# Decode attention with a gated mixer: PV with V as the moving operand, by hand on TensorE

## The chip, the cores and the metric

The kernel runs on one NeuronCore of a Trainium2 chip. The metric is the device time of one execution in microseconds; the median of several runs counts. The engines are named as in the profile: PE (TensorE, with PEld for its weight loads), DVE (VectorE), ACT (ScalarE), POOL (GpSimd) and SP (SyncE, which here only issues transfers). Sixteen DMA engines move data from the main memory (HBM) into the on-chip memory (SBUF). Matmul results go to PSUM.

## What is computed

One new token of width 512 passes through an attention block (32 heads, a cache of 16,384 keys and values per head, head width 128) and, beside it, through a small gated mixer. A scalar gate mixes the two results.

```python
x = A_x                                             # (1, 1, 512)
g = sigmoid((x * gate_w).sum(-1, keepdims=True))

# attention
q = (x @ wq).reshape(1, 1, 32, 128).transpose(0, 2, 1, 3)
scores = einsum('bhqd,bhkd->bhqk', q, k_cache) * 128 ** -0.5
p = softmax(scores)
o = einsum('bhqk,bhkd->bhqd', p, v_cache)
a = o.transpose(0, 2, 1, 3).reshape(1, 1, 4096) @ wo

# mixer (one token)
z = gelu(einsum('bsd,df->bsf', x, w_in))            # 1792 wide
z1, z2 = z[..., :896], layernorm(z[..., 896:])
b = einsum('bsf,fd->bsd', z1 * (w_sp * z2 + b_sp), w_out)

return g * a + (1 - g) * b                          # (1, 1, 512)
```

All inputs are bf16. K and V of one head have 4 MB (4,194,304 bytes) each, so the caches are 64 such loads; wq and wo are another 4 MB each, w_in and w_out 1.8 and 0.9 MB.

## The kernel before

A K or V tile has 128 partitions. Partition p holds the keys p*128 to p*128+127, each with 128 elements, so that every partition reads one run of 32 KB. The whole program is unrolled: no loop is left on the chip.

*Start.* wq is loaded into a buffer of the v tag (L69), then K of heads 0 to 2, V of head 0 and the mixer's weights (L97 to L106). The query is computed with x spread over all columns of the stationary operand, so that every partition has the whole q (`qb`, L116 to L126).

*Scores of head h (`scores`, L210 to L226).* K is done in two halves of 64 keys per partition. VectorE multiplies a half by q in place (L216). PE adds the products up over groups of 8 elements: 16 matmuls with the identity as stationary operand and 512 columns add slices of the product into one PSUM bank (L219). VectorE reduces the remaining 8 (L221). ACT takes the exponent of both halves at once and the row sums with it (L224). The softmax is taken without a maximum; the sums are divided out at the end.

*PV of head h (`attend`, L228 to L232).* 128 matmuls: each loads a block of V (128 keys x 128 elements) as stationary operand and sends one column of p through it. They add up in column h of `o_ps`, which is o in columns.

*Order.* The loop at L237 runs over the heads, two heads ahead with the scores: it loads K of h+2, computes the scores of h+2, loads V of h, and does PV of h. The framework puts each engine's instructions into an order by priority, which follows the program, and by what it takes to be ready; it adds the semaphores itself. K has three buffers and V two (wq and wo take part: wq in a v buffer, wo in a k buffer). All large loads go through SP's queue in one order: V of h waits until PV of h-2 has freed its buffer, and K of h+3 is queued behind V of h+1. The gate (L141) and the mixer (L159) are called after head 1.

*End.* V of head 31 is loaded in three pieces (64, 32 and 32 blocks), wo in three (16, 12 and 4 slices of 512 columns, L253). The sum of all exponents comes from a matmul with ones (L258), o is normalised (L265) and turned from columns into the order in which wo's rows lie on the partitions: a PE transpose (L267), a copy (L269) and four matmuls with a selection matrix (L272). Then 128 matmuls with wo as stationary operand (L278) add to `a_ps`, in which the mixer's part already stands (L204). In each the stationary operand takes every fourth column of wo (`"p (k m c) -> p k m c"`, L255), so that element 4m+c of the output lies in partition m, column c. The result (128 x 4) is cast (L281) and written with 128 runs of 8 bytes (L282).

Of the kernel before, what the change touches and what calls it, by code (L numbers as in the profile page):

```python
# [8 lines left out]
ACT = mybir.ActivationFunctionType  # L9
ALU = mybir.AluOpType  # L10
AX = mybir.AxisListType

FP32 = mybir.dt.float32
BF16 = mybir.dt.bfloat16
# [3 lines left out]
def kernel(  # L18
# [57 lines left out]
    def load_k(h):  # L76
        t = kv.tile([P, NJ * Dh], BF16, name="k_t", tag="k", bufs=3)
        nc.sync.dma_start(out=t[:], in_=k_src[h])  # L78
        ktile[h] = t

    def load_v(h, cuts=()):
        t = kv.tile([P, NJ * Dh], BF16, name="v_t", tag="v")
        edges = [0, *cuts, NJ]
        for a, b in zip(edges[:-1], edges[1:]):
            nc.sync.dma_start(out=t[:, a * Dh:b * Dh], in_=v_src[h][:, a * Dh:b * Dh])  # L85
        vtile[h] = t
# [43 lines left out]
    for i in range(4):  # L130
        nc.vector.tensor_copy(out=sel[:, i, :].rearrange("h (m i) -> h m i", i=4)[:, :, i],
                              in_=ident[0:H, 0:H])

    a_ps = ps_1.tile([P, 512], FP32, name="a_ps")
    o_ps = ps_1.tile([P, H], FP32, name="o_ps")
    g_sb = const.tile([P, 1], FP32, name="g_sb")
# [4 lines left out]
    def gate():  # L141
        gw_ps = ps_m.tile([P, DC + 2], FP32, name="gw_ps", tag="mm")
        for c in range(DC):
            nc.tensor.matmul(gw_ps[:, c:c + 1], lhsT=gw_row[0:1, c::DC], rhs=ones_row[0:1, 0:1],
                             start=True, stop=True)
        nc.tensor.matmul(gw_ps[:, DC:DC + 2], lhsT=ones_row[0:1, :], rhs=wb_row[0:1, :],  # L146
                         start=True, stop=True)
        gw_col = const.tile([P, DC], BF16, name="gw_col")
        nc.vector.tensor_copy(out=gw_col[:], in_=gw_ps[:, 0:DC])  # L149
        nc.vector.tensor_copy(out=wbf[:], in_=gw_ps[:, DC:DC + 2])  # L150
        g_ps = ps_m.tile([P, 1], FP32, name="g_ps", tag="mm")
        for c in range(DC):
            nc.tensor.matmul(g_ps[:, :], lhsT=xb[:, c, :], rhs=gw_col[:, c:c + 1],
                             start=(c == 0), stop=(c == DC - 1))
        nc.scalar.activation(out=g_sb[:], in_=g_ps[:, :], func=ACT.Sigmoid)
        nc.scalar.activation(out=gm_sb[:], in_=g_ps[:, :], func=ACT.Sigmoid, scale=-1.0)


    def mixer():  # L159
        z_ps = ps_m.tile([P, FC], FP32, name="z_ps", tag="mm")  # L160
        w_in5 = w_in[:].rearrange("p c (e m k) -> p c e m k", e=2, k=FhC)
        for fc in range(FC):
            for c in range(DC):
                nc.tensor.matmul(z_ps[:, fc:fc + 1], lhsT=w_in5[:, c, fc // FhC, :, fc % FhC],  # L164
                                 rhs=xb[:, c, 0:1], start=(c == 0), stop=(c == DC - 1))
        z = const.tile([P, FC], FP32, name="z")
        nc.vector.tensor_copy(out=z[:], in_=z_ps[:])  # L167
        t = const.tile([P, FC], FP32, name="t")
        nc.vector.tensor_mul(out=t[:], in0=z[:], in1=z[:])
        nc.vector.tensor_scalar(out=t[:], in0=t[:], scalar1=0.044715, scalar2=1.0,  # L170
                                op0=ALU.mult, op1=ALU.add)
        nc.vector.tensor_mul(out=t[:], in0=t[:], in1=z[:])
        nc.scalar.activation(out=t[:], in_=t[:], func=ACT.Sigmoid, scale=1.5957691216057308)
        nc.vector.tensor_mul(out=z[:], in0=z[:], in1=t[:])
        stats = const.tile([P, 2], FP32, name="stats")
        nc.vector.reduce_sum(out=stats[:, 0:1], in_=z[:, FhC:FC], axis=AX.X)
        sq = const.tile([P, FhC], FP32, name="sq")
        nc.vector.tensor_mul(out=sq[:], in0=z[:, FhC:FC], in1=z[:, FhC:FC])
        nc.vector.reduce_sum(out=stats[:, 1:2], in_=sq[:], axis=AX.X)
        tot_ps = ps_m.tile([P, 2], FP32, name="tot_ps", tag="mm")  # L180
        nc.tensor.matmul(tot_ps[:, :], lhsT=ones_f[:, :], rhs=stats[:, :], start=True, stop=True)
        mv = const.tile([P, 2], FP32, name="mv")
        nc.vector.tensor_scalar(out=mv[:], in0=tot_ps[:, :], scalar1=1.0 / Fh, scalar2=0.0,
                                op0=ALU.mult, op1=ALU.add)
        var = const.tile([P, 1], FP32, name="var")
        nc.vector.tensor_mul(out=var[:], in0=mv[:, 0:1], in1=mv[:, 0:1])
        nc.vector.tensor_sub(out=var[:], in0=mv[:, 1:2], in1=var[:])
        rstd = const.tile([P, 1], FP32, name="rstd")
        nc.scalar.activation(out=rstd[:], in_=var[:], func=ACT.Sqrt, bias=eps_t[:, 0:1], scale=1.0)
        nc.vector.reciprocal(out=rstd[:], in_=rstd[:])  # L190
        z2n = const.tile([P, FhC], FP32, name="z2n")
        nc.vector.tensor_scalar(out=z2n[:], in0=z[:, FhC:FC], scalar1=mv[:, 0:1],
                                scalar2=rstd[:, 0:1], op0=ALU.subtract, op1=ALU.mult)
        nc.vector.tensor_scalar(out=z2n[:], in0=z2n[:], scalar1=wbf[:, 0:1],
                                scalar2=wbf[:, 1:2], op0=ALU.mult, op1=ALU.add)
        uf = const.tile([P, FhC], FP32, name="uf")
        nc.vector.tensor_mul(out=uf[:], in0=z[:, 0:FhC], in1=z2n[:])
        u = const.tile([P, FhC], BF16, name="u")
        nc.vector.tensor_scalar(out=u[:], in0=uf[:], scalar1=gm_sb[:, 0:1], scalar2=0.0,  # L199
                                op0=ALU.mult, op1=ALU.add)  # L200
        w_out4 = w_out[:].rearrange("p k (m c) -> p k m c", c=DC)
        for k in range(FhC):
            for c in range(DC):
                nc.tensor.matmul(a_ps[:, c:c + 1], lhsT=w_out4[:, k, :, c], rhs=u[:, k:k + 1],  # L204
                                 start=(k == 0 and c == 0), stop=False, skip_group_check=True)

    L_sb = const.tile([P, H], FP32, name="L_sb")
    p_sb = {}

    def scores(h):  # L210
        k3 = ktile[h][:].rearrange("p (j d) -> p j d", d=Dh)
        qh = qb[:, h * Dh:(h + 1) * Dh].unsqueeze(1).broadcast_to([P, NH, Dh])
        s_sb = sp.tile([P, NJ], FP32, name="s_sb")
        for s in range(2):
            ks = k3[:, s * NH:(s + 1) * NH, :]
            nc.vector.tensor_tensor(out=ks, in0=ks, in1=qh, op=ALU.mult)  # L216
            s_ps = ps_s.tile([P, NH, W], FP32, name="s_ps")
            for i in range(NS):
                nc.tensor.matmul(s_ps[:, :, :], lhsT=ident[:, :], rhs=ks[:, :, i * W:(i + 1) * W],  # L219
                                 start=(i == 0), stop=(i == NS - 1))  # L220
            nc.vector.tensor_reduce(out=s_sb[:, s * NH:(s + 1) * NH], in_=s_ps[:, :, :],  # L221
                                    axis=AX.X, op=ALU.add)
        p_t = sp.tile([P, NJ], BF16, name="p_t", bufs=4)
        nc.scalar.activation(out=p_t[:], in_=s_sb[:], func=ACT.Exp, scale=inv_sqrt_dh,  # L224
                             accum_out=L_sb[:, h:h + 1])
        p_sb[h] = p_t  # L226

    def attend(h):  # L228
        v3 = vtile[h][:].rearrange("p (j d) -> p j d", d=Dh)
        for j in range(NJ):  # L230
            nc.tensor.matmul(o_ps[:, h:h + 1], lhsT=v3[:, j, :], rhs=p_sb[h][:, j:j + 1],  # L231
                             start=(j == 0), stop=(j == NJ - 1))  # L232

    AHEAD = 2
    scores(0)
    scores(1)
    for h in range(H):  # L237
        if h + AHEAD < H:
            if h > 0:
                load_k(h + AHEAD)  # L240
            scores(h + AHEAD)
        if h > 0:
            load_v(h, cuts=(64, 96) if h == H - 1 else ())
        if h < H - 1:
            attend(h)
        if h == 1:
            gate()
            mixer()


    wo_t = kv.tile([P, H * D], BF16, name="wo_t", tag="k", bufs=3)
    wo_src = A_wo.rearrange("(p k) n -> p (k n)", k=H)
    for a, b in ((0, 16), (16, 28), (28, 32)):  # L253
        nc.sync.dma_start(out=wo_t[:, a * D:b * D], in_=wo_src[:, a * D:b * D])  # L254
    wo4 = wo_t[:].rearrange("p (k m c) -> p k m c", k=H, c=DC)  # L255

    ltot_ps = ps_m.tile([P, H], FP32, name="ltot_ps", tag="mm")
    nc.tensor.matmul(ltot_ps[:, :], lhsT=ones_f[:, :], rhs=L_sb[:, :], start=True, stop=True)  # L258
# [16 lines left out]
    nc.vector.tensor_copy(out=o2[:], in_=o2_ps[:, :])  # L275
    for k in range(H):
        for c in range(DC):
            nc.tensor.matmul(a_ps[:, c:c + 1], lhsT=wo4[:, k, :, c], rhs=o2[:, k:k + 1],  # L278
                             start=False, stop=(k == H - 1), skip_group_check=True)
    res = const.tile([P, DC], BF16, name="res")  # L280
    nc.vector.tensor_copy(out=res[:], in_=a_ps[:, 0:DC])  # L281
    nc.sync.dma_start(out=out.rearrange("a b (p c) -> (a b p) c", c=DC), in_=res[:])  # L282


# [28 lines left out]
```

## Time and profile before

| quantity | us |
|---|---|
| median of 8 runs | 667.06 (666.7 to 667.64) |
| the profiled execution | 667.01 |
| its span, first to last instruction | 665.1 |
| PE busy on scores (L219), all heads | 289.5 |
| PE busy on PV (L231), all heads | 108.4 |
| VectorE busy on products (L216), all heads | 280.5 |
| one half of a product (L216) | 4.42 |
| reducing one half (L221) | 0.69 |
| PV of one head, matmuls (L231) | 3.35 |
| a V load, from issue to landing (median) | 32.3 |
| a K load, from issue to landing (median) | 41.7 |

The span is what the profiler sees between the first and the last instruction. Busy times of different engines overlap and don't add up to the span. Where the profile says "clock 0.50", PE's clock was granted at half its full rate in that stretch. "x16" is the number of instructions merged into a row. In the profile's rows, an arrow with a name at the end tells what ended the wait before it.

In the steady part a head looks like this on the engines (head 29 of 0 to 31, in us from the span's start): K has landed by 580.65, VectorE multiplies until 589.41, PE does the scores from 585.13 to 594.54, PV of head 27 follows from 594.38, and SP issues V of head 29 at 597.82.

### The profile page before, as it was taken

The numbers are of one execution on the slowest core, as the hardware profiler recorded it, in microseconds if no ns is written. First come the engines' busy times: TensorE is split into PE (matmuls) and PEld (weight loads), VectorE is DVE, ScalarE is ACT, GpSimd is POOL, SyncE is SP. The second block draws the span as 40 slices with busy tenths as digits, with TensorE's granted clock in tenths as the row PEclk, the third lists the DMA queues.
The fourth block names the chain that finished last, engine by engine and source line by source line (L and its number), as shares of the span: only waits on it lengthen the run. The fifth ranks groups of instructions, "written<-read, shape, count | busy, mean of one in ns | idle before, by whom it ended". The sixth has DMA issues, their size and how long they took to land.

```text
span 665.1 us, 11264 instructions
## 1 busy us (share of the span) xinstructions
PE 412.9 (62%) x5386; PEld 237.4 (36%) x5386; DVE 330.9 (50%) x162; ACT 25.5 (4%) x81; POOL 0.7 (0%) x6
## 2 busy tenths in 40 slices
PE   2767656567756567664557765557775654776663
PEld 1325333334323334422334432334442333442363
DVE  1593655444655444565544465544455653456500
ACT  0402000000000000000000000000000000000000
POOL 0000000000000000000000000000000000000000
PEclk9898666787656787866787876677876668876665
DMA  9999999999999999999999999999999999999985
GB/s 378 441 429 429 431 429 431 433 426 430 435 427 433 424 435 433 427 431 435 425 431 436 423 429 438 429 427 432 431 428 436 425 430 431 431 432 434 399 353 229
DMA packets 10566, 280.31 MB, mean 421 GB/s; under 512 B 1302, under 2 KB 1304, under 8 KB 1560
## 3 DMA queue, kind: packets, MB, share of 16 engines
q1 hardware_dynamic: 10512, 279.58, 98.0%
q8 instruction: 42, 0.69, 0.4%
q14 instruction: 4, 0.03, 0.0%
q10 hardware_dynamic: 8, 0.00, 0.0%
HBM read 279.58 MB, written 0.00 MB: 420 GB/s over the span
## 4 chain that ended last, share of the span: by engine, by line
DMA 69%; PE 20%; DVE 9%; SPq 1%; issue 0%; DVEq 0%
DMA k_t<-in_A_k_cache_dram 66%; PE s_ps L219 15%; DVE k_t L216 9%; PE o_ps L231 5%; DMA wo_t<-in_A_wo_dram 3%; SPq L85 1%; PE a_ps L278 0%; DVE s_sb L221 0%; SPq L254 0%; SPq L69 0%; PE ltot_ps L258 0%; DVE res L281 0%; SPq L78 0%; DVEq L216 0%
## 5 line engine op out<-in xcount | busy, mean ns | idle before, releaser
L219 PE MATMUL s_ps<-k_t,ident 128*128 128x512 bf16 x1024 | 289.5, 452 | 219.1 <-DVE k_t L216 219.1
L216 DVE TENSOR_TENSOR k_t<-k_t,qb 128x8192 bf16<-128x8192 bf16 x64 | 280.5, 4421 | 149.7 <-DMA k_t<-in_A_k_cache_dram 149.7
L219 PEld LDWEIGHTS <-ident 128*128 128x128 bf16 x1024 | 115.3, 113 | 381.1 <-issue 222.7
L231 PEld LDWEIGHTS <-v_t 128*128 128x128 bf16 x4096 | 108.3, 97 | 14.2 <-DMA v_t<-in_A_v_cache_dram 7.1
L231 PE MATMUL o_ps<-p_t,v_t 128*128 128x1 bf16 x4096 | 108.4, 163 | 6.7 <-DMA v_t<-in_A_v_cache_dram 6.7
L221 DVE TENSOR_REDUCE s_sb<-s_ps 128x64 f32<-128x512 f32 x64 | 44.2, 691 | 127.3 <-PE s_ps L219 127.3
L224 ACT ACTIVATE p_t<-s_sb 128x128 bf16<-128x128 f32 x32 | 9.9, 310 | 586.1 <-DVE s_sb L221 586.1
L121 PE MATMUL q_ps<-wq_t,xb 128*128 128x512 bf16 x32 | 8.8, 443 | 10.3 <-DMA wq_t<-in_A_wq_dram 10.3
L121 PEld LDWEIGHTS <-xb 128*128 128x128 bf16 x32 | 3.5, 110 | 15.4 <-issue 11.7
L278 PE MATMUL a_ps<-o,wo_t 128*128 128x1 bf16 x128 | 4.6, 172 | 4.9 <-DMA wo_t<-in_A_wo_dram 4.9
L265 DVE TENSOR_TENSOR o_sb<-o_ps,rl 128x32 bf16<-128x32 f32 x1 | 0.2, 190 | 13.6 <-PE o_ps L231 13.6
L278 PEld LDWEIGHTS <-wo_t 128*128 128x128 bf16 x128 | 4.4, 118 | 5.1 <-DMA wo_t<-in_A_wo_dram 5.1
L124 DVE CAST qb<-q_ps 128x512 bf16<-128x512 f32 x1 | 0.7, 691 | 11.1 <-PE q_ps L121 11.1
L224 ACT ACTIVATION_READ_ACCUMULATOR p_t<-s_sb 128x1 f32 x32 | 6.0, 187 | 0.0
L281 DVE CAST res<-a_ps 128x4 bf16<-128x4 f32 x1 | 0.2, 163 | 9.3 <-PE a_ps L278 9.3
L126 ACT CAST qb<-q_ps 128x512 bf16<-128x512 f32 x7 | 4.1, 585 | 14.9 <-PE q_ps L121 14.9
L149 DVE CAST gw_col<-gw_ps 128x4 bf16<-128x4 f32 x1 | 0.2, 163 | 6.5 <-PE gw_ps L146 6.5
L164 PE MATMUL z_ps<-xb,w_in 128*128 128x1 bf16 x56 | 3.1, 192 | 0.0
L164 PEld LDWEIGHTS <-w_in 128*128 128x128 bf16 x56 | 3.1, 154 | 0.0
L167 DVE COPY z<-z_ps 128x14 f32<-128x14 f32 x1 | 0.2, 172 | 5.5 <-PE z_ps L164 5.5
L224 ACT ACT_TABLE_LOAD x2 | 2.6, 1283 | 0.0
L204 PE MATMUL a_ps<-u,w_out 128*128 128x1 bf16 x28 | 1.1, 172 | 2.3 <-DVE u L199 2.3
(57 smaller groups left out, 18.7 us busy)
## 6 DMA issues: line engine op xcount, KB each, us to landing
k_t<-in_A_k_cache_dram SPq DMA_DIRECT2D x32, 4096.0 KB, 41.7
v_t<-in_A_v_cache_dram SPq DMA_DIRECT2D x31, 4096.0 KB, 32.8
wq_t<-in_A_wq_dram SPq DMA_DIRECT2D x1, 4096.0 KB, 12.2
v_t<-in_A_v_cache_dram SPq DMA_DIRECT2D x1, 2048.0 KB, 7.8
v_t<-in_A_v_cache_dram SPq DMA_DIRECT2D x2, 1024.0 KB, 10.5
wo_t<-in_A_wo_dram SPq DMA_DIRECT2D x1, 2048.0 KB, 16.7
w_in<-in_B_w_in_dram SPq DMA_DIRECT2D x1, 1792.0 KB, 44.4
wo_t<-in_A_wo_dram SPq DMA_DIRECT2D x1, 1536.0 KB
```

The lines of the kernel that those rows point to most:

```text
L85: nc.sync.dma_start(out=t[:, a * Dh:b * Dh], in_=v_src[h][:, a * Dh:b * Dh])
L121: nc.tensor.matmul(q_ps[:, :], lhsT=xb[:, c, :], rhs=wq[:, c, nb * QB:(nb + 1) * QB], start=(c == 0), stop=(c == DC - 1))
L124: nc.vector.tensor_copy(out=qb[:, 0:QB], in_=q_ps[:, :])
L126: nc.scalar.copy(out=qb[:, nb * QB:(nb + 1) * QB], in_=q_ps[:, :])
L164: nc.tensor.matmul(z_ps[:, fc:fc + 1], lhsT=w_in5[:, c, fc // FhC, :, fc % FhC], rhs=xb[:, c, 0:1], start=(c == 0), stop=(c == DC - 1))
L204: nc.tensor.matmul(a_ps[:, c:c + 1], lhsT=w_out4[:, k, :, c], rhs=u[:, k:k + 1], start=(k == 0 and c == 0), stop=False, skip_group_check=True)
L216: nc.vector.tensor_tensor(out=ks, in0=ks, in1=qh, op=ALU.mult)
L219: nc.tensor.matmul(s_ps[:, :, :], lhsT=ident[:, :], rhs=ks[:, :, i * W:(i + 1) * W], start=(i == 0), stop=(i == NS - 1))
L221: nc.vector.tensor_reduce(out=s_sb[:, s * NH:(s + 1) * NH], in_=s_ps[:, :, :], axis=AX.X, op=ALU.add)
L224: nc.scalar.activation(out=p_t[:], in_=s_sb[:], func=ACT.Exp, scale=inv_sqrt_dh, accum_out=L_sb[:, h:h + 1])
L231: nc.tensor.matmul(o_ps[:, h:h + 1], lhsT=v3[:, j, :], rhs=p_sb[h][:, j:j + 1], start=(j == 0), stop=(j == NJ - 1))
L278: nc.tensor.matmul(a_ps[:, c:c + 1], lhsT=wo4[:, k, :, c], rhs=o2[:, k:k + 1], start=False, stop=(k == H - 1), skip_group_check=True)
```

## The change

- `attend` stays for heads 29 to 31. For heads 0 to 28 it is replaced by `attend_wide` and `collect`. `attend_wide` takes four columns of p as stationary operand (128 x 4) and four blocks of V as moving operand (128 x 512); 32 such matmuls add up in a PSUM tile `d_ps` of 4 x 512. Row r of the tile holds the sum of p's columns 4g+r with all four blocks; only the diagonal blocks (row r, columns r*128 to r*128+127) belong together. ACT copies the tile to SBUF. `collect`, one head later, adds the four diagonal blocks into column h of `o_ps` with four fp32 matmuls against a 4 x 4 identity (`ident_f`, a new tile copied at the start).
- The scores are cut into halves (`scores_half`), with the same instructions.
- PE's instructions in the loop keep the order in which the program states them: first half of the scores of h+2, `collect` of h-1, second half, `attend_wide` of h. For head 29, `attend` stands between the two halves of head 31's scores. Gate and mixer follow `attend_wide` of head 1.
- V of h is now requested before the scores of h+2 in the program. V of head 31 is requested after the loop.
- wo is loaded in four pieces, of 16, 8, 6 and 2 slices. The stationary operands from w_out and wo are blocks of 128 adjacent columns, so that element 128c+m of the output lies in partition m, column c. A PE transpose turns the result into 4 rows of 128, a VectorE copy moves it to SBUF, and the output is written with 4 runs of 256 bytes.

```diff
+    ident_f = const.tile([4, 4], FP32, name="ident_f")
+    nc.vector.tensor_copy(out=ident_f[:], in_=ident[0:4, 0:4])
...
-        w_out4 = w_out[:].rearrange("p k (m c) -> p k m c", c=DC)
+        w_out4 = w_out[:].rearrange("p k (c m) -> p k c m", c=DC)
...
-                nc.tensor.matmul(a_ps[:, c:c + 1], lhsT=w_out4[:, k, :, c], rhs=u[:, k:k + 1],
+                nc.tensor.matmul(a_ps[:, c:c + 1], lhsT=w_out4[:, k, c, :], rhs=u[:, k:k + 1],
...
+    R = 512 // Dh
+    diag = {}
+
+    def attend_wide(h):
+        d_ps = ps_s.tile([R, R * Dh], FP32, name="d_ps")
+        NG = NJ // R
+        for g in range(NG):
+            nc.tensor.matmul(d_ps[:, :], lhsT=p_sb[h][:, g * R:(g + 1) * R],
+                             rhs=vtile[h][:, g * R * Dh:(g + 1) * R * Dh],
+                             start=(g == 0), stop=(g == NG - 1))
+        d_sb = sp.tile([R, R * Dh], FP32, name="d_sb")
+        nc.scalar.copy(out=d_sb[:], in_=d_ps[:, :])
+        diag[h] = d_sb
+
+    def collect(h):
+        for r in range(R):
+            nc.tensor.matmul(o_ps[:, h:h + 1], lhsT=diag[h][:, r * Dh:(r + 1) * Dh],
+                             rhs=ident_f[:, r:r + 1], start=(r == 0), stop=(r == R - 1))
+
     AHEAD = 2
-    scores(0)
-    scores(1)
-    for h in range(H):
-        if h + AHEAD < H:
+    WIDE = H - 3
+    with tc.manual_schedule(engines={mybir.EngineType.PE}):
+        for h in range(AHEAD):
+            scores_half(h, 0)
+            scores_half(h, 1)
+        for h in range(H - 1):
             if h > 0:
-                load_k(h + AHEAD)
-            scores(h + AHEAD)
-        if h > 0:
-            load_v(h, cuts=(64, 96) if h == H - 1 else ())
-        if h < H - 1:
-            attend(h)
-        if h == 1:
-            gate()
-            mixer()
+                if h + AHEAD < H:
+                    load_k(h + AHEAD)
+                load_v(h)
+            if h + AHEAD < H:
+                scores_half(h + AHEAD, 0)
+            if 0 < h <= WIDE:
+                collect(h - 1)
+            if h < WIDE:
+                scores_half(h + AHEAD, 1)
+                attend_wide(h)
+            else:
+                attend(h)
+                if h + AHEAD < H:
+                    scores_half(h + AHEAD, 1)
+            if h == 1:
+                gate()
+                mixer()
+        load_v(H - 1, cuts=(64, 96))
...
-    for a, b in ((0, 16), (16, 28), (28, 32)):
+    for a, b in ((0, 16), (16, 24), (24, 30), (30, 32)):
...
-            nc.tensor.matmul(a_ps[:, c:c + 1], lhsT=wo4[:, k, :, c], rhs=o2[:, k:k + 1],
+            nc.tensor.matmul(a_ps[:, c:c + 1], lhsT=wo4[:, k, c, :], rhs=o2[:, k:k + 1],
...
-    nc.sync.dma_start(out=out.rearrange("a b (p c) -> (a b p) c", c=DC), in_=res[:])
+    rT_ps = ps_m.tile([DC, P], BF16, name="rT_ps", tag="mm")
+    nc.tensor.transpose(rT_ps[:, :], res[:], ident[:])
+    resT = const.tile([DC, P], BF16, name="resT")
+    nc.vector.tensor_copy(out=resT[:], in_=rT_ps[:, :])
+    nc.sync.dma_start(out=out.rearrange("a b (c m) -> (a b c) m", c=DC), in_=resT[:])
```

More of the change, by code (lines that the diff above doesn't have):

```diff
@@ L208, with scores_half @@
     p_sb = {}
-    def scores(h):
+    s_tile = {}
+    def scores_half(h, s):
         k3 = ktile[h][:].rearrange("p (j d) -> p j d", d=Dh)
         qh = qb[:, h * Dh:(h + 1) * Dh].unsqueeze(1).broadcast_to([P, NH, Dh])
[L213 to L226, printed above, removed]
+        if s == 0:
+            s_tile[h] = sp.tile([P, NJ], FP32, name="s_sb")
+        s_sb = s_tile[h]
+        ks = k3[:, s * NH:(s + 1) * NH, :]
+        nc.vector.tensor_tensor(out=ks, in0=ks, in1=qh, op=ALU.mult)
+        s_ps = ps_s.tile([P, NH, W], FP32, name="s_ps")
+        for i in range(NS):
+            nc.tensor.matmul(s_ps[:, :, :], lhsT=ident[:, :], rhs=ks[:, :, i * W:(i + 1) * W],
+                             start=(i == 0), stop=(i == NS - 1))
+        nc.vector.tensor_reduce(out=s_sb[:, s * NH:(s + 1) * NH], in_=s_ps[:, :, :],
+                                axis=AX.X, op=ALU.add)
+        if s == 1:
+            p_t = sp.tile([P, NJ], BF16, name="p_t", bufs=4)
+            nc.scalar.activation(out=p_t[:], in_=s_sb[:], func=ACT.Exp, scale=inv_sqrt_dh,
+                                 accum_out=L_sb[:, h:h + 1])
+            p_sb[h] = p_t
     def attend(h):
@@ L251 @@
     wo_t = kv.tile([P, H * D], BF16, name="wo_t", tag="k", bufs=3)
     wo_src = A_wo.rearrange("(p k) n -> p (k n)", k=H)
-    for a, b in ((0, 16), (16, 28), (28, 32)):
+    for a, b in ((0, 16), (16, 24), (24, 30), (30, 32)):
         nc.sync.dma_start(out=wo_t[:, a * D:b * D], in_=wo_src[:, a * D:b * D])
-    wo4 = wo_t[:].rearrange("p (k m c) -> p k m c", k=H, c=DC)
+    wo4 = wo_t[:].rearrange("p (k c m) -> p k c m", k=H, c=DC)
     ltot_ps = ps_m.tile([P, H], FP32, name="ltot_ps", tag="mm")
```

## The prediction

> **What bounds the kernel now.** I read the busy table first, then the slices, the queue table, the chain of waits, the stages and the order of time at the end.
>
> ```profile
> PE 412.9 (62%) x5386; PEld 237.4 (36%) x5386; DVE 330.9 (50%) x162; ACT 25.5 (4%) x81; POOL 0.7 (0%) x6
> DMA  9999999999999999999999999999999999999985
> GB/s 378 441 429 429 431 429 431 433 426 430 435 427 433 424 435 433 427 431 435 425 431 436 423 429 438 429 427 432 431 428 436 425 430 431 431 432 434 399 353 229
> ...
> q1 hardware_dynamic: 10512, 279.58, 98.0%
> q8 instruction: 42, 0.69, 0.4%
> ...
> DMA 69%; PE 20%; DVE 9%; SPq 1%; issue 0%; DVEq 0%
> ```
>
> No compute engine is full, the 16 DMA engines are in every slice but two, and the chain is 69% transfers. A pair of k and v tiles (8.39 MB) at 431 GB/s takes 19.4 us, the period of a head in the chain (58.2 us per three heads). The chain also shows PE and VectorE 29% of the time, but that is no bound: a v load issued at 557.09 lands a median of 32.3 us later, because two and a bit transfers of 9.7 us are queued ahead of it. About 22 us of queued work therefore covers the path "k lands, product, scores, PV, next v load".
>
> ```profile
> core 0: us, PE busy (x) PEld busy (x) DVE busy (x) ACT busy (x) POOL busy (x), PEclk, DMA share, GB/s
> 622.00:630.00 8.00, 6.03 (x21) 2.40 (x21) 6.85 (x3) 0.00 (x0) 0.00 (x0) 0.66 1.02 438
> 630.00:633.00 3.00, 3.00 (x30) 1.59 (x29) 0.31 (x2) 0.00 (x0) 0.00 (x0) 1.00 0.43 186
> 633.00:636.00 3.00, 3.00 (x119) 3.00 (x116) 0.47 (x1) 0.40 (x2) 0.00 (x0) 1.00 0.61 262
> 636.00:639.00 3.00, 0.27 (x5) 0.16 (x5) 0.60 (x2) 0.00 (x0) 0.00 (x0) 0.78 0.76 279
> 639.00:655.00 16.00, 7.93 (x261) 7.40 (x261) 0.59 (x3) 0.00 (x0) 0.00 (x0) 0.50 1.00 421
> ```
>
> The stage from 630 to 637 is where the loss shows: half of the DMA engines idle. The packet records of the trace say which half. Each load is 128 packets of 32 KB, eight per engine, 1.215 us each. At 630.2 to 631.2 eight engines end v of head 30; the other eight end it at 637.0 to 638.4, some 7 us later, and run on into v of head 31 (issued at 636.3) without a gap. So the late eight are never idle and set the end; an earlier v load alone would only move idle time of the early eight. What makes them late is the other queue: each of the 42 instruction packets (16 KB, about 1.05 us) holds up one engine, and its next data packet takes about 1.7 us instead of 1.215. A fetch costs its engine about 1.05 + 0.5 = 1.55 us. 42 x 1.55 / 8 = 8.1 us, which is the lag. The 42 fetches are TensorE's: 2 x 5386 = 10,772 instructions of 64 bytes are 0.69 MB.
>
> ```profile
> 655.03 2.29 PE L278 MATMUL a_ps<-o,wo_t 128*128 128x1 bf16 x64 [3.51 <-DMA wo_t<-in_A_wo_dram]
> ...
> 658.73 2.29 PE L278 MATMUL a_ps<-o,wo_t 128*128 128x1 bf16 x64 [1.41 <-DMA wo_t<-in_A_wo_dram]
> 661.06 0.16 DVE L281 CAST res<-a_ps 128x4 bf16<-128x4 f32 x1 [9.31 <-PE a_ps L278]
> 661.25 0.35 SPq L282 DMA_DIRECT2D out_dram<-res  x1
> ```
>
> The last data packet ends at 659.49. The second wo piece releases 64 matmuls at 658.73 (the third piece has landed before they are through), and the sum is there at 661.04, 1.55 us after the last packet.
>
> **What the Trainium skill says.** "Runtime: NRT & Kernel Launch", section Instruction fetch mechanics: an engine's instructions are streamed in 16 KiB blocks of 256 by a DMA queue of its sequencer, and the cost is "mostly hidden". The 42 packets of 16 KB agree; hidden it is only from TensorE, for here the DMA engines are the bound. "DMA: Bandwidth & Descriptors", section Queues, rings and completion order: a transfer is split over fixed rings of the 16 engines, and an engine takes turns between rows. That agrees with a lag that never evens out. "TensorE: Matmul & The Clock Gate", Part 1: the clock is half when TensorE has idled for some 3.4 us and full after as long of activity. The trace agrees: 0.50 between heads, 1.00 at the end of the scores; matmuls of 512 columns start 0.426 us apart at first and about 0.216 apart warm (16 in 3.61 us, the last one's latency included).
>
> **The change, part by part.** The profiled execution took 667.01 us for a span of 665.1, so about 1.9 us lie outside; the median of the runs is 667.06, and I carry differences over to it.
>
> *V as moving operand, heads 0 to 28.* Removed: 29 x 128 matmuls with a weight load each. Added: 29 x 32 matmuls of 512 columns, 29 x 4 fp32 ones (two instructions each, as ltot's x2 rows show) and 29 ACT copies (0.58 us by the q copies, on an engine 4% busy: nothing). TensorE's matmuls become 1024 + 928 + 232 + 384 (three narrow heads) + 267 (rest) = 2835, with weight loads 5670 instructions, 22 fetches. 20 fetches fewer x 1.55 / 8 engines = 3.9 us on the late half. Fetches come whole: the latest engine had about 6 of 42 and will have 3 of 22, 4.7 us. I take 4.2; bounds 2.5 (the rest falls unevenly) and 6 (no lag matters).
>
> TensorE pays per head: first half 16 x 0.216 = 3.5 us warm, 6.8 cold; collect 8 small fp32 instructions, 0.6 to 2.4 us by the ltot and tot rows, taken 1; second half 3.5; wide PV 32 x 0.216 = 6.9. That is 14.9 to 18.2 us in a period of 19.4: below the transfers, and shorter idle keeps it warmer. Its cover is narrow, and the rival below prices its loss. VectorE keeps its 2 x 4.42 + 2 x 0.69 = 10.2 us. From k landing to the v buffer coming free: 8.9 us of products, some 5 for the second half behind collect, 6.9 wide = about 20.9, against 16.9 (4.4 + 9.2 + 3.3). The next v and k loads are issued 4 us later, with about 18 us of transfers still queued: hidden. SP's order stays v of h, then k of h+3.
>
> *TensorE by hand.* Gate and mixer now stand after the wide PV of head 1 (at 89 us or so), with some 9 us of round trips to VectorE and ACT while the scores of head 4 queue behind. Before, that block ran in idle time. It delays the next v load by perhaps 6 to 12 us with over 12 queued: nothing; if VectorE puts 4.4 us products between, up to 3 us are lost.
>
> *The last heads.* PV of head 29 goes between the halves of head 31, so v of head 31 is issued one second half (3.4 us) earlier, at about 630 with everything 3.6 us sooner. The late engines don't wait for it; it removes idle time of the early ones and keeps a reserve: nothing by itself. What is late next is still the late half.
>
> *wo in 16, 8, 6, 2, contiguous blocks.* Bytes and packets' time stay (about 9.9 us). After the last packet 8 matmuls are due, not a backlog of 64. The third piece's last packets end 0.66 us before the end, its 24 matmuls start 0.49 us after (as at 658.23 to 658.72) and take 24 x 0.028 (the spacing of PV with contiguous blocks; wo strided has 0.036): the sum is there some 0.87 us after the last packet instead of 1.55. Gain 0.65; bounds 0 and 1.1.
>
> *Rows by a transpose.* Added on the open end: transpose and copy, as at oT: 0.06 + 0.29 + 0.03 + 0.21 = 0.6 us. The output becomes 4 packets of 256 bytes for 128 of 8. Those took 0.2 us in all of the 3.9 us from the issue to the end; the rest is latency. No row shows the new form: gain between 0 and 0.8, taken 0.3. The copy for ident_f runs at the start with VectorE idle: nothing.
>
> Sum: -4.2 - 0.65 + 0.6 - 0.3 = -4.55; 667.06 - 4.55 = 662.5 us.
>
> **The rivals.**
> A. Forecast, the lag shrinks with the fetches: 662.5, own range 660.8 to 665.
> B. The fetches are no lever, or the start or the block at head 1 gives the gain back: the tail alone, -0.65 + 0.6 - 0.3, 666.7. For it: only 0.4% of DMA time is fetches. Against: the lag and the fetch count agree.
> C. Slower: TensorE becomes the bound in the wide PV. If a stationary operand of 4 columns doesn't count as activity, the clock falls during it: half the 32 matmuls at 0.426 make it 10.3 us, the next head starts cold (6.8), and with 1 + 4.4 a head takes 22.5. Beyond 19.4 it decides: 3.1 x 29 = 90 us more, 757. For it: TensorE's busy time goes from 12.4 to over 15 us per head, and no row here has a narrow stationary operand. Against: PV with one moving column kept the clock at 1.00 (633 to 636).
>
> **How the numbers follow.** A measurement tells about 0.2% (1.3 us) from no change. A 0.75, B 0.14, C 0.11. Of A, 0.02 lies above 665.7; of B, 0.02 lies below and 0.02 above the bounds. Faster 0.73 + 0.02 = 0.75, same 0.02 + 0.10 = 0.12, slower 0.11 + 0.02 = 0.13. The range for 8 in 10 leaves C out, takes A's bounds, and reaches to B: 660.6 to 667.0.
>
> **What would show it.** Right: about 22 instruction packets, late engines 3 to 4.5 us behind, v of head 31 issued near 630, the last wo packet near 655.3, sum within 1 us of it, TensorE's clock above 0.9 in mid heads. Wrong: a fetch count near 40; a DMA share below 0.95 between 100 and 600; v loads waiting for TensorE with no transfer queued; a first wide PV at clock 0.50.

## The result, and the profile after

The changed kernel takes 662.72 us (median of 10 runs, 661.53 to 663.97) against 667.24 us: a ratio of 0.9933, 95% interval 0.9925 to 0.9941. That is 4.5 us less. (The forecast started from 667.06 us, the median of the first 8 runs of the kernel before; 667.24 is that of 28.) The profiled execution took 661.57 us with a span of 659.7, so it is one of the quickest of the ten; that matters below, because the runs of the changed kernel lie twice as far apart as those of before.

From the page of the changed kernel: the busy table, the DMA engines' share and rate in 40 slices, the DMA queues and the chain of waits.

```profile
PE 525.5 (80%) x2835; PEld 233.4 (35%) x2835; DVE 329.8 (50%) x164; ACT 39.5 (6%) x108; POOL 0.7 (0%) x6
DMA  9999999999999999999999999999999999999995
GB/s 382 435 422 433 433 438 418 429 425 440 425 433 432 425 436 432 430 433 428 431 430 435 425 435 432 429 432 431 428 429 437 428 433 430 431 428 435 428 412 244
...
q1 hardware_dynamic: 10520, 279.58, 98.8%
q8 instruction: 22, 0.36, 0.2%
...
DMA 60%; PE 30%; DVE 9%; SPq 1%; issue 0%; ACT 0%; DVEq 0%
```

TensorE is busier than before (80% for 62%) with half the instructions, the bytes are the same, the rate in the middle is the same (430 and 431 GB/s between 160 and 600 us), and the instruction packets are 22 where there were 42. Whatever was gained was not gained by a faster steady part.

The end, by stages (the columns are those of the table shown before):

```profile
628.00:631.00 3.00, 3.00 (x65) 1.95 (x62) 0.00 (x0) 0.00 (x0) 0.00 (x0) 0.69 0.96 399
631.00:634.00 3.00, 3.00 (x12) 1.24 (x11) 0.00 (x0) 0.00 (x0) 0.00 (x0) 0.74 0.97 399
634.00:637.00 3.00, 1.41 (x23) 0.81 (x22) 1.29 (x3) 0.40 (x2) 0.00 (x0) 1.00 0.95 407
637.00:651.00 14.00, 7.37 (x249) 6.84 (x245) 0.60 (x3) 0.00 (x0) 0.00 (x0) 0.58 0.99 416
```

The stretch in which half of the DMA engines idled (a share of 0.43 to 0.76 between 630 and 639) has gone: 0.95 and more. And in order of time, the last instructions of the changed kernel:

```profile
653.89 1.01 PE L317 MATMUL a_ps<-o,wo_t 128*128 128x1 bf16 x32 [0.57 <-DMA wo_t<-in_A_wo_dram]
655.76 1.02 PE L317 MATMUL a_ps<-o,wo_t 128*128 128x1 bf16 x32 [0.86 <-DMA wo_t<-in_A_wo_dram]
656.82 0.16 DVE L320 CAST res<-a_ps 128x4 bf16<-128x4 f32 x1 [8.06 <-PE a_ps L317]
657.03 0.27 PE L322 MATMUL rT_ps<-ident,res 128*4 128x128 bf16 x1 [0.25 <-DVE res L320]
657.34 0.21 DVE L324 COPY resT<-rT_ps 4x128 bf16<-4x128 bf16 x1 [0.36 <-PE rT_ps L322]
657.58 0.35 SPq L325 DMA_DIRECT2D out_dram<-resT  x1
```

The transpose costs 0.6 us here, as the oT pair did. But from the output's issue to the end of the span there are 2.1 us (657.58 to 659.7), where there were 3.9 (661.25 to 665.1).

The packet records of the trace tell the rest. They don't name the engine of a packet. But each engine closes its share of a load with a 4-byte packet for the semaphore, so there are sixteen end times for each load. Two columns of the table give when the sixteen engines end v of head 30, the early eight and the late eight; then comes the last packet of weights, and what lies between it and the span's end. The table holds kernels of the experiments too.

| kernel | instruction packets | early half, us | late half, us | last weights packet | from there to the end |
|---|---|---|---|---|---|
| before | 42 | 630.0 to 631.5 | 636.7 to 638.4 | 659.49 | 5.65 |
| changed | 22 | 630.4 to 632.6 | 633.6 to 636.0 | 655.93 | 3.78 |
| tail_only | 42 | 630.5 to 631.6 | 636.4 to 638.6 | 659.46 | 3.79 |
| narrow_order | 42 | 630.3 to 631.6 | 636.8 to 638.3 | 659.31 | 3.83 |
| wide_only | 22 | 631.9 to 632.9 | 633.8 to 637.9 | 657.60 | 5.60 |
| wide_cut4 | 44 | 633.2 to 634.4 | 639.4 to 641.5 | 661.27 | 3.84 |
| mixer_early | 22 | 630.3 to 632.8 | 633.5 to 635.6 | 655.33 | 3.80 |

On average the late eight are 7.2 us behind the early eight before and 3.3 us in the changed kernel.

### The profile page after: what moved, and what is told of

Its sections match the earlier page's. It is cut to its first block, busy times and chain, and to the rows that moved or that the text cites. A ratio compares the mean times of both kernels' runs of the same rounds, so it can differ in the third digit from the quotient of the medians.

```text
span 659.7 us, 6195 instructions
## 1 busy us (share of the span) xinstructions
PE 525.5 (80%) x2835; PEld 233.4 (35%) x2835; DVE 329.8 (50%) x164; ACT 39.5 (6%) x108; POOL 0.7 (0%) x6
## 4 chain that ended last, share of the span: by engine, by line
DMA 60%; PE 30%; DVE 9%; SPq 1%; issue 0%; ACT 0%; DVEq 0%
DMA k_t<-in_A_k_cache_dram 52%; PE s_ps L225 15%; PE d_ps L250 12%; DVE k_t L222 8%; DMA v_t<-in_A_v_cache_dram 4%; DMA wo_t<-in_A_wo_dram 4%; PE o_ps L259 2%; SPq L85 1%; PE o_ps L239 1%; PE z_ps L167 0%; PE a_ps L317 0%; SPq L293 0%; PE a_ps L207 0%; PE tot_ps L184 0%; SPq L69 0%
## 5 line engine op out<-in xcount | busy, mean ns | idle before, releaser
L225 PE MATMUL s_ps<-k_t,ident 128*128 128x512 bf16 x1024 | 265.7, 419 | 95.4 <-DVE k_t L222 95.4
L250 PE MATMUL d_ps<-v_t,p_t 128*4 128x512 bf16 x928 | 205.0, 379 | 0.0
L225 PEld LDWEIGHTS <-ident 128*128 128x128 bf16 x1024 | 105.7, 106 | 241.3 <-issue 145.0
L250 PEld LDWEIGHTS <-p_t 128*4 128x4 bf16 x928 | 76.4, 85 | 126.1 <-issue 12.3
L259 PEld LDWEIGHTS o_ps<-ident_f,d_sb 4*128 4x128 f32 x232 | 27.9, 186 | 12.3 <-issue 12.3
L259 PE MATMUL o_ps<-ident_f,d_sb 4*128 4x1 f32 x232 | 30.4, 248 | 0.0
L254 ACT COPY d_sb<-d_ps 4x512 f32<-4x512 f32 x29 | 16.7, 574 | 170.7 <-PE d_ps L250 170.7
L239 PE MATMUL o_ps<-p_t,v_t 128*128 128x1 bf16 x384 | 10.7, 164 | 4.9 <-DMA v_t<-in_A_v_cache_dram 4.9
L239 PEld LDWEIGHTS <-v_t 128*128 128x128 bf16 x384 | 10.2, 99 | 5.3 <-DMA v_t<-in_A_v_cache_dram 5.3
L207 PE MATMUL a_ps<-u,w_out 128*128 128x1 bf16 x28 | 0.9, 165 | 10.4 <-DVE u L202 10.4
L124 DVE CAST qb<-q_ps 128x512 bf16<-128x512 f32 x1 | 0.7, 690 | 11.3 <-PE q_ps L121 11.3
L207 PEld LDWEIGHTS <-w_out 128*128 128x128 bf16 x28 | 1.1, 111 | 10.4 <-issue 10.4
```

Source lines behind the costliest of these rows:

```text
L250: nc.tensor.matmul(d_ps[:, :], lhsT=p_sb[h][:, g * R:(g + 1) * R], rhs=vtile[h][:, g * R * Dh:(g + 1) * R * Dh], start=(g == 0), stop=(g = ...
L254: nc.scalar.copy(out=d_sb[:], in_=d_ps[:, :])
L259: nc.tensor.matmul(o_ps[:, h:h + 1], lhsT=diag[h][:, r * Dh:(r + 1) * Dh], rhs=ident_f[:, r:r + 1], start=(r == 0), stop=(r == R - 1))
```

## The experiments

The theory of the prediction (theory 1) says that every instruction packet of TensorE delays one of some eight DMA engines by about 1.55 us, and that these late engines set the end. Its rivals: TensorE's order and clock bring the gain (theory 2), or the end of the kernel does. Times are medians. The runs were made in three groups, each on one chip, in which the kernel before had 667.42 us (pv_twice, wide_cut4, wide_only, tail_only), 667.51 (mixer_split, mixer_split_cut4, narrow_order, rows_out) and 667.12 (mixer_early, mixer_early_w30). A comparison across groups is therefore uncertain by some 0.4 us.

Two counts in the packet records bear on theory 1 directly. First, slow packets: between 160 and 600 us, 29 of the 5,761 data packets of 32 KB took over 1.3 us in the kernel before, 15 in the changed one and 51 in pv_twice, and in the same stretch TensorE fetched 28, 13 and 49 instruction packets. Nearly all the others take 1.21 to 1.23 us, so nothing else that TensorE does slows the transfers there to speak of. Second, which engines: in narrow_order the engines can be followed from load to load between 407 us and the end of v of head 30. An engine's eight packets of a load take 9.73 us; fifteen times they took 11.2 to 11.3, each time with an instruction packet in between, and all fifteen lie on the eight engines that end last, one or two on each.

**More packets on the kernel before (pv_twice).**

```diff
+    again_ps = ps_1.tile([P, H], FP32, name="again_ps")
...
+        if h < H - 3:
+            for j in range(NJ):
+                nc.tensor.matmul(again_ps[:, h:h + 1], lhsT=v3[:, j, :], rhs=p_sb[h][:, j:j + 1],
+                                 start=(j == 0), stop=(j == NJ - 1))
```

> The kernel before, with the 128 PV matmuls of heads 0 to 28 issued a second time into a PSUM column that nothing reads. Theory 1 (instruction packets delay half of the DMA engines): 7,424 more TensorE instructions are 29 more packets, 71 in all; 29 x 1.55 / 8 = 5.6 us more, 672.8 us, and the late engines some 14 us behind at the end of head 30's v. Theory 2 (the gain came from TensorE's order and clock, instruction count is free): TensorE has 15.7 us of work in a period of 19.4, the v loads are issued 3.3 us later with some 22 us queued; 667.2 us, no change.

Measured: 673.33 us, ratio 1.0088 (1.0074 to 1.0102), 5.9 us more. From its page, the queue of instruction packets:

```profile
q8 instruction: 71, 1.16, 0.7%
```

The late half ends v of head 30 at 642.7 to 644.9 instead of 636.7 to 638.4. Theory 1 had 5.6 us; theory 2 had nothing. TensorE's added work itself is hidden (the DMA share between 160 and 600 is 1.00). The lag of 14 us that was expected can't be read off: the early eight had run dry before, near 621, and waited for this load until about 629, so they end it at 638.9 to 639.3.

**The same columns in four times as many matmuls (wide_cut4).**

```diff
-        for g in range(NG):
-            nc.tensor.matmul(d_ps[:, :], lhsT=p_sb[h][:, g * R:(g + 1) * R],
-                             rhs=vtile[h][:, g * R * Dh:(g + 1) * R * Dh],
-                             start=(g == 0), stop=(g == NG - 1))
+        for r in range(R):
+            for g in range(NG):
+                j = g * R + r
+                nc.tensor.matmul(d_ps[:, r * Dh:(r + 1) * Dh], lhsT=p_sb[h][:, g * R:(g + 1) * R],
+                                 rhs=vtile[h][:, j * Dh:(j + 1) * Dh],
+                                 start=(g == 0), stop=(g == NG - 1))
```

> The changed kernel, with each wide PV matmul of 512 columns cut into four of 128 columns: the same columns streamed, the same order and waits, the same tail, but about 5,570 more instructions, 43 to 44 packets instead of 22. Theory 1: 21 x 1.55 / 8 = 4.1 us more than the changed kernel, 666.8 us. Theory 2: TensorE's time per head stays near 15 to 18 us and hidden, 662.7 us as the changed kernel.

Measured: 667.09 us, 4.4 us more than the changed kernel; the whole gain is gone with the columns streamed, the order, the end and TensorE's mean clock (0.91) unchanged. From its page:

```profile
q8 instruction: 44, 0.72, 0.4%
```

But the table shows something that theory 1 doesn't contain: the early half is late too, by 3 us against before. Its stages between 110 and 150:

```profile
110.00:122.00 12.00, 12.00 (x86) 6.72 (x85) 3.15 (x3) 1.68 (x3) 0.00 (x0) 0.86 0.99 426
122.00:130.00 8.00, 8.00 (x101) 6.04 (x98) 6.89 (x2) 0.58 (x2) 0.00 (x0) 1.00 0.78 305
130.00:150.00 20.00, 20.00 (x194) 13.49 (x192) 10.74 (x5) 0.97 (x3) 0.00 (x0) 1.00 0.99 424
```

Between 122 and 130 the DMA share (the last column but one) is 0.78: some 1.8 us of all 16 engines are lost there. So this run mixes two costs, and they are taken apart below.

**The parts by themselves (wide_only, tail_only).** wide_only is the changed kernel with the end of before; tail_only is the kernel before with the end of the changed one.

```diff
 # wide_only, against the changed kernel
-    for a, b in ((0, 16), (16, 24), (24, 30), (30, 32)):
+    for a, b in ((0, 16), (16, 28), (28, 32)):
-    wo4 = wo_t[:].rearrange("p (k c m) -> p k c m", k=H, c=DC)
+    wo4 = wo_t[:].rearrange("p (k m c) -> p k m c", k=H, c=DC)
...
-    nc.sync.dma_start(out=out.rearrange("a b (c m) -> (a b c) m", c=DC), in_=resT[:])
+    nc.sync.dma_start(out=out.rearrange("a b (p c) -> (a b p) c", c=DC), in_=res[:])
```

> The changed kernel with the end of before (wo in three pieces, strided columns, output of 128 runs). Theory 1: the lag's part alone, 22 packets, 667.2 - 4 = 663.2 us. Rival (the end brings most of it): 666 us or more.

Measured: 664.98 us, ratio 0.9962 (0.9949 to 0.9976): 2.4 us less than before, 1.8 short of what theory 1 expected. Its DMA share between 120 and 130 is 0.92, and its early half is 1.5 to 2 us late.

> The kernel before with the end of the changed kernel (wo in four pieces, contiguous blocks, output as 4 rows after a transpose) and nothing else; 42 packets. Theory 1: 0.65 for the shorter rest of matmuls, 0.6 paid for the transpose, and the output transfer 0.3 (prediction) to 1.75 (one profile of the changed kernel) shorter: 665.4 to 666.9 us. Rival (the end brings most of it): 663 us.

Measured: 665.04 us, ratio 0.9966 (0.9954 to 0.9979): 2.4 us less than before. The end is worth far more than the 0.35 us of the prediction, and wide_only's 20 packets are worth less than 4. The last packet of weights comes when it came before (659.46); what lies behind it is 1.86 us shorter in the profiled executions, which are 2.0 us apart.

**Where the end's gain lies (rows_out).** The kernel before with contiguous blocks and rows, wo in its three pieces:

```diff
-    wo4 = wo_t[:].rearrange("p (k m c) -> p k m c", k=H, c=DC)
+    wo4 = wo_t[:].rearrange("p (k c m) -> p k c m", k=H, c=DC)
...
+    nc.tensor.transpose(rT_ps[:, :], res[:], ident[:])
+    nc.vector.tensor_copy(out=resT[:], in_=rT_ps[:, :])
+    nc.sync.dma_start(out=out.rearrange("a b (c m) -> (a b c) m", c=DC), in_=resT[:])
```

> The kernel before with contiguous blocks and the output as 4 rows of 256 bytes after a transpose; wo in three pieces as before. If the output transfer's end brings 1.5 us, less 0.6 for transpose and copy, and the contiguous loads some 0.3: about 666.0 us, and from the output packets to the span's end 1.3 us instead of 2.8. If the transfer brings nothing: 667.5 us.

Measured: 665.76 us, ratio 0.9976 (0.9967 to 0.9986). From the last output packet to the end of the span it has 1.34 us; the kernel before, pv_twice and wide_only, with 128 runs of 8 bytes, have 2.85, 2.81 and 2.78, and all kernels with rows 1.28 to 1.34. In all of them about 1.0 us of it is the program's own end. SyncE's wait for the output shows the difference (before, then the changed kernel; in all, times, longest):

```profile
SPq L308 <- DMA out_dram<-res: 2.4, 1, 2.4
...
SPq L351 <- DMA out_dram<-resT: 0.7, 1, 0.7
```

In the trace's semaphore records the first of the 16 confirmations of the 128 runs comes 0.2 us after the last packet and the last one 1.8 us after it; the rows have four, and the last comes after 0.33 us. So the transfer of 4 runs of 256 bytes is confirmed 1.5 us sooner. The number of runs, their length and the number of engines (4 for 16) changed together, and no run takes them apart.

The blocks of wo bring something too. The last 64 matmuls of rows_out:

```profile
659.02 1.86 PE L278 MATMUL a_ps<-o,wo_t 128*128 128x1 bf16 x64 [1.83 <-DMA wo_t<-in_A_wo_dram]
```

With every fourth column they took 2.29 us (the line at 658.73 of before). From the last packet of weights to the sum there are 1.55 us in the kernel before, 1.10 in rows_out and 0.86 in tail_only: the contiguous blocks bring 0.45 us, the fourth piece of wo 0.24. The medians of rows_out and tail_only lie 0.7 us apart, but these are of two groups of runs, and only 0.3 us of it is found behind the last packet of weights.

**TensorE's order alone (narrow_order).**

```diff
-    WIDE = H - 3
+    WIDE = -1
```

> The changed kernel with the old PV for all heads, between the two halves of the scores: TensorE's order by hand and the new end, but 42 packets. Theory 1: the order brings nothing, so the time is that of before with the new end alone, 665.0 us. Theory 2 (order and earlier v loads bring it): about 662.7 us.

Measured: 665.15 us, ratio 0.9964 (0.9952 to 0.9976): that of tail_only. The order by hand, with PV between the two halves of the scores and v of head 31 asked for sooner, brings nothing by itself. That leaves TensorE's clock: its mean here is 0.78, for 0.74 before and 0.91 in the changed kernel. But wide_cut4 had the changed kernel's clock and order, and no gain. With the two runs theory 2 falls.

**The dip near 125 us (mixer_split, mixer_split_cut4, mixer_early).** In the changed kernel, in order of time (a row's brackets give the idle time before it):

```profile
95.65 0.56 PE L184 MATMUL tot_ps<-stats,ones_f 128*128 128x2 f32 x2 [1.90 <-DVE stats L182]
...
96.71 4.42 DVE L222 TENSOR_TENSOR k_t<-k_t,qb 128x8192 bf16<-128x8192 bf16 x1
...
101.04 0.16 DVE L193 RECIPROCAL rstd<-rstd 128x1 f32<-128x1 f32 x1
101.12 4.41 DVE L222 TENSOR_TENSOR k_t<-k_t,qb 128x8192 bf16<-128x8192 bf16 x1
...
106.57 0.89 PE L207 MATMUL a_ps<-u,w_out 128*128 128x1 bf16 x28 [10.37 <-DVE u L202]
...
107.32 5.07 PE L225 MATMUL s_ps<-k_t,ident 128*128 128x512 bf16 x16
...
123.96 0.33 SPq L85 DMA_DIRECT2D v_t<-in_A_v_cache_dram  x1
```

The mixer's chain on VectorE has two products of 4.4 us between its small steps. TensorE waits 10.4 us for it, and the scores of head 4, whose first product was ready at 101.1, start at 107.32 behind the mixer's last matmuls. The v load that depends on the next PV goes out at 123.96, when the DMA engines have just about emptied their queues (near 125.5); their packets after it take up to 1.98 us instead of 1.215. In this execution, a quick one, three engines stop for a moment and the DMA share between 122 and 130 is still 0.96. With the same wait, the load goes out at 125.26 in wide_only and at 126.77 in wide_cut4; there nearly all engines or all of them stand idle, until about 126.3 and 127.8. The slower executions of the changed kernel itself were not profiled.

mixer_split cuts the mixer at its two waits into stages after heads 1, 2 and 3:

```diff
                 gate()
-                mixer()
+                mixer_a()
+            if h == 2:
+                mixer_b()
+            if h == 3:
+                mixer_c()
```

> The changed kernel, with the mixer cut into three stages that follow the wide PV of heads 1, 2 and 3 in TensorE's order, so that no scores wait behind a round trip to VectorE. Theory H (the block at head 1 lets all 16 DMA engines run dry near 125 us): the dip of the DMA share between 110 and 130 goes, and the time is what packets and end give together, 667.3 - 4.0 - 1.9 = 661.4 us, with less spread between runs. Rival (the dip costs only the early engines, which have time to lose): 662.7 us as the changed kernel.

Measured: 661.28 us, ratio 0.9905 (0.9891 to 0.9919), runs of 660.81 to 662.33. mixer_split_cut4 adds the cut of wide_cut4 to it:

> The same, with each wide PV matmul cut into four of 128 columns: 44 instruction packets instead of 22 with no dip to confuse the reading. Theory 1: 22 x 1.55 / 8 = 4.3 us more than with 22 packets, some 665.5 us. Theory 2 (count is free): the same time as the one with 22.

Measured: 666.21 us, ratio 0.9987 (0.9979 to 0.9995): 4.9 us more for 22 packets more. Neither is wholly free of dips. In mixer_split the v loads go out at 118.74 and 143.43; before the second the queues are nearly empty again, and between 144.8 and 147.9 fourteen packets take 1.3 to 1.8 us; in mixer_split_cut4 ten packets between 142.0 and 146.6 take 1.4 to 2.1 us. So the three stages shrank the dip and moved it. mixer_early moves the block whole:

```diff
-            if h == 1:
+            if h == 0:
                 gate()
                 mixer()
```

> The changed kernel with gate and mixer one head earlier, after the wide PV of head 0, where TensorE idles some 9.9 us in the changed kernel's trace (63.7 to 73.5) and no scores wait behind them. Theory H: no dip of the DMA share before 160, the next v loads 8 us and more sooner, 661.2 us or a little less, spread as before's. If the three-stage version left nothing to gain: 661.3 us, the same spread as it. If the dip costs nothing: 662.7 us.

Measured: 660.82 us, ratio 0.9901 (0.9884 to 0.9917), the quickest version of all with mixer_early_w30; its four runs lie within 0.3 us. In order of time:

```profile
63.76 3.12 PE L167 MATMUL z_ps<-xb,w_in 128*128 128x1 bf16 x56
...
68.78 0.56 PE L184 MATMUL tot_ps<-stats,ones_f 128*128 128x2 f32 x2 [1.90 <-DVE stats L182]
...
71.62 0.89 PE L207 MATMUL a_ps<-u,w_out 128*128 128x1 bf16 x28 [2.28 <-DVE u L202]
75.94 4.99 PE L225 MATMUL s_ps<-k_t,ident 128*128 128x512 bf16 x16 [3.44 <-DVE k_t L222]
...
108.69 0.33 SPq L85 DMA_DIRECT2D v_t<-in_A_v_cache_dram  x1
```

Here the block lies in an idle stretch: its last wait is 2.28 us instead of 10.37, and TensorE still waits 3.44 us for the next product after it. The v load that went out at 123.96 goes out at 108.69, and no bunch of slow packets is left between 100 and 160.

**A little less at the end (mixer_early_w30).**

```diff
+            if h == H - 2:
+                attend_wide(h)
...
+    collect(H - 2)
     attend(H - 1)
```

> The same, and PV of head 30 wide too: some 180 TensorE instructions less, 0.7 of a packet, all of it in the last 40 us. Theory 1: 0.1 us less, or up to 1.5 where the packet that goes had hit the engine that ends last; a loss of up to 1 us if TensorE's slow clock makes the wide PV (7 to 14 us) late for the pieces of head 31's v.

Measured: 660.83 us, no difference from mixer_early. The 0.1 us expected can't be told from nothing; the larger gain and the loss didn't come.

## Why the prediction came out, and which terms were off

The forecast was 662.5 us and the measured time is 662.72, a change of -4.55 us forecast and -4.5 measured. The largest term was right, and for the reason given. But two other terms were wrong by 1.9 and 1.5 us, in opposite directions. That the sum came out this close is luck.

- *V as moving operand: -4.2 us.* Right. With no dip in either, tail_only (42 packets) against mixer_early (22) is 665.04 against 660.82: 4.2 us for 20 packets (3.9 when each is set against the kernel before of its own group). The mechanism is shown by pv_twice (5.9 us for 29 more) and mixer_split_cut4 (4.9 for 22 more), with TensorE's work hidden in both. Spread over eight engines, that is 1.6 to 1.8 us a packet, a little over the 1.55 that was forecast and the 1.5 by which the fifteen turns in narrow_order are longer; what the rest is, no run shows. The late half is 3.3 us behind instead of 7.2, inside the forecast of 3 to 4.5. The forecast's lag of 8.1 us for all 42 packets was a little too long: 39 of them come before v of head 30 has ended, and 39 x 1.5 / 8 = 7.3; the changed kernel has 19 until then, 3.6.
- *TensorE's time per head.* Right, and rival C with its fallen clock is out: the wide PV takes 7.07 us for 32 matmuls (predicted 6.9) at a clock of 1.00, and TensorE needs 15.4 us per head (17.0 where the first half starts at the slow clock) of a period of 19.4. Here, a stationary operand of four columns kept the clock up.
- *The block at head 1: "nothing; ... up to 3 us are lost".* The step named the mechanism and its price, and then chose nothing. It costs 1.9 us (662.72 for 660.82 in mixer_early; 1.8 against each group's kernel before). The mis-sized term is the wait: VectorE did put its products between the steps, so the next v load went out at 123.96, with next to nothing left of the queue that was to cover it. It may also explain the wider spread, since the load comes within a microsecond or two of the queues' end. That isn't shown: mixer_early's four runs lie within 0.3 us, but the fourteen of mixer_split_cut4, without this wait, spread over 2.5 us.
- *v of head 31 sooner: nothing by itself.* Right: narrow_order is equal to tail_only.
- *wo in four contiguous pieces: -0.65 us.* Right: from the last packet of weights to the sum there are 0.9 us (655.93 to 656.82) where 0.87 was worked out. The larger part of the gain, 0.45 us, comes from the contiguous blocks and 0.24 from the fourth piece.
- *Rows by a transpose: +0.6 - 0.3 us.* The cost was right and the gain was not: from the issue to the span's end 1.8 us are saved, not 0.3, outside even the upper bound of 0.8. The prediction took nearly all but the packets' own 0.2 us for a latency that both forms would share. Some 1.0 us of it, the program's end, is shared. The wait for the confirmation is not: after the last output packet it is 1.8 us with 128 runs of 8 bytes and 0.33 with 4 runs of 256. The Trainium skill, "DMA: Bandwidth & Descriptors", section Anatomy of one DMA, which is about transfers issued by GpSimd, says that most of a roughly constant cost of about 2 us is the wait for the target memory's receipt, HBM's being the heaviest. For this output, which SyncE issues, the 1.8 us of the small runs are of that size; that the wait is constant doesn't hold, since it was 0.33 in the other form. Why the small runs are confirmed later, no run here shows.

The sum by these runs: -4.2 (packets) - 2.4 (the whole end) + 1.9 (dip) = -4.7 us; measured -4.5. The three are differences along one row of kernels, so they must add up, but for the groups' offsets. An independent check is wide_only (packets and dip, -2.4) with tail_only (the end, -2.4): -4.8. The first half of rival B, by which packets are no lever, is refuted by pv_twice and by mixer_split_cut4; its second half, that the block at head 1 gives gain back, came true for 1.9 of 4.2 us.

Still open: why the packets fall on eight of the sixteen DMA engines only, and whether instruction packets of other engines than TensorE would cost the same. Neither was tried.

## What to carry to other kernels

Where the DMA engines are the bound, look at what else they carry: the program's own instructions come through them, and a busiest engine with many tiny instructions can cost time without ever being on the chain of waits. A block with round trips between engines belongs where the in-order engine is idle anyway, and is to be priced by what is issued behind it, not by its own length. The last transfer of a kernel has its price in what follows the last packet: it is worth trying to write a small result in few long runs, which here saved 1.5 us for a transpose and a copy of 0.6.

## What the runs showed of the hardware that was not expected

- A transfer of 1 KB to HBM was confirmed 1.8 us after its last packet when it consisted of 128 runs of 8 bytes, and 0.33 us after it when it consisted of 4 runs of 256 bytes, in all profiles taken.
- An instruction packet of 16 KB takes nearly as long as a data packet of 32 KB (1.05 us against 1.215), and the next data packet on that engine mostly takes 1.7 us. Where the engines could be followed (narrow_order), TensorE's packets came on eight of the sixteen DMA engines only.
- In wide_cut4 all sixteen DMA engines stood idle for a moment near 127 us, and their first 32 KB packets after it took 1.4 to 2.1 us instead of 1.215, so the dip cost more than the idle time in it. In the changed kernel's profile, where the queues nearly ran empty, such packets took up to 1.98 us.
